# Moving the fifth expert block's second product ahead of a branch, and computing the third block in split precision

## Chip, cores and metric

One core of one Trainium2 chip runs the whole program. The metric is the device time of one execution in microseconds (us); lower is better. The kernel before takes 602.93 us in the median of three runs.

## What is computed

Attention over 4 batches and 8 heads feeds a first mixture of experts, and that feeds a second one. The change lies in the second one alone, whose 2304 tokens of 512 numbers are dealt to 8 experts of at most 288 tokens each:

```python
logits = x @ w_gate
for idx in np.argsort(-logits.flatten()):      # best (token, expert) pairs first
    tok, e = idx // E, idx % E
    if assigned[tok] < 0 and counts[e] < 288:
        assigned[tok] = e; counts[e] += 1
for e in range(8):
    h = np.maximum(x[assigned == e] @ w1[e], 0.0)
    out[assigned == e] = h @ w2[e]
```

## The kernel before

**Two strands.** After the first mixture (about 285 us into the span) two strands run interleaved until the end. The *search* settles the experts one after the other, in eight phases. A phase (`phase`) takes six steps to find the score at which an expert is full. Each step is a comparison `G` on VectorE (DVE), 18 small matmuls `pc` on TensorE (PE), a count `sat` and `an` on DVE, one small matmul `pa<-an` on PE and the next threshold `th` on DVE. A phase ends with the prefix count `pp` (PE) and `sc`, `sl`, `alive` (DVE). Then `ilist` makes the list of the expert's tokens (DVE `si`, `ol`, `OH`, `rh`, PE `pl`, DVE `li`, `ib`), and GpSimd (POOL) gathers those rows into `xg` (line 982). The last three experts first pass through `ahead` (DVE `mk`, `mksb`, PE `pk`), which sorts out tokens that need no computing, and through a small count `pz`, from which DVE works out a flag `zi`.

**Blocks.** The other strand computes the experts in the order in which the search settles them, block 0 to block 7. `first(m)` is x·w1 with ReLU: 8 groups (f) of 4 products of 128x128 by 128x288. `second(m)` is h·w2: 4 groups (d) of 8 such products. Blocks below `LATE` (0, 1 and 2) run in plain fp32. The trace has such a product as two MATMUL rows (`pa<-x,w1b`, `pa<-h,w2b`). From block `LATE` on, operands are split into a high and a low fp32r part (`xhs`/`xls`, `hhs`/`hls`, `w1hs`/`w1ls`, `w2hs`/`w2ls`), and a product is three fp32r matmuls. The split costs ScalarE (ACT) a copy and DVE a subtraction for each part: `sp1(m,k)` four times for w1, during `second(m-1)`; `sp2(m,k)` four times for w2, during `first(m)`; `xls` four times in `X(m,d)`, which brings the gathered rows of the next block into place by transposes `pt` during `second(m-1)`; `hls` eight times. Transposes `pt` and those of the outputs, `py`, share a pool of two PSUM buffers, and `pt` is free again when `xhs` and `xls` have read it.

**What sets the order.** All engines run their instructions in program order. A planner (`Search.tick`, `step`, `after`) sets that order when the program is built: it keeps a reckoned time of PE (`Q.pe`) and of DVE (`Q.dv`), and puts the next piece of the search in between block products when PE's reckoned time has come up to it. So PE's row of instructions says how many block products stand between two steps of the search.

**The branch.** `Q.until` finishes the search, `z=nc.values_load(K.zi...)` (line 1179) loads the flag on every engine, and `tc.If(z>1)` chooses `short()` when the last expert computes nothing and two others hold at most 160 tokens. These inputs take `short()`: it writes zero rows by five scatters from POOL, runs `second(4)` with `X`-like transposes `xin(5,d)` in between (lines 1119 to 1124), then blocks 5 and 6 in plain fp32 with 160 columns (lines 1132 and 1144), and ends. Loads of w1 and w2 for block 5 are issued by SyncE (SP) once the expert's number is out (`eb`); those for block 6 follow.

Of the kernel before, what the change touches and what calls it, by code (L numbers as in the profile page):

```python
# [7 lines left out]
F32 = mybir.dt.float32  # L8
# [11 lines left out]
E = 8  # L20
# [978 lines left out]

BUB=5  # L1000
FEW=160
LATE=3


def moe2(nc,tc,t,K,W,Q,yd,w1,w2,out):
    V=Q.V; G=nc.gpsimd; T=Q.T
    with ExitStack() as ctx:
        c=ctx.enter_context(tc.tile_pool(name="m2c",bufs=1))
        b2=ctx.enter_context(tc.tile_pool(name="m2b",bufs=2))
        acc=ctx.enter_context(tc.tile_pool(name="m2a",bufs=4,space=PSUM))  # L1010
        pst=ctx.enter_context(tc.tile_pool(name="m2p",bufs=2,space=PSUM))
        psr=ctx.enter_context(tc.tile_pool(name="m2r",bufs=2,space=PSUM))
        R=Q.B; tick=Q.tick; K.zi=None
# [3 lines left out]
        sw=[c.tile(x,F32R,name=f"{n}s") for n,x in (("w1h",[128,4,1024]),("w1l",[128,4,1024]),("w2h",[128,8,512]),("w2l",[128,8,512]))]  # L1017
# [5 lines left out]
        def sp1(m,k):  # L1023
            sp(0,Q.w1b[m%2],slice(k,k+1),k)
            if k==3: R[m].f1=True; Q.loads()
# [3 lines left out]
        def X(m,d):  # L1029
            r=R[m]  # L1030
            if d==0 and m<LATE: r.x=b2.tile([128,4,CAP],F32,name="x2",bufs=1)
            pt=pst.tile([128,288],F32,name="pt2",tag="t")
            for u in range(3): T.transpose(pt[:,96*u:96*u+96],r.xg[:,u,128*d:128*d+128],K.ident[:96,:96])
            if m<LATE: nc.scalar.copy(r.x[:,d],pt)
            else: nc.scalar.copy(xs[0][:,d],pt); Q.after(0.6); V.tensor_tensor(xs[1][:,d],pt,xs[0][:,d].bitcast(F32),op=ALU.subtract)
            tick()
# [14 lines left out]
        def mul(m,pa,z,k,sl,first,last):  # L1051

            if m<LATE:
                T.matmul(pa,(Q.w1b,Q.w2b)[z][m%2][:,k,sl],(R[m].x,hT)[z][:,k],start=first,stop=last); tick()
# [3 lines left out]
        def first(m):  # L1058
            r=R[m]; Q.blk=m
            for f in range(8):  # L1060

                if m==LATE and f>3: sp2(m,f-4)
                elif m>LATE and f%2==0: sp2(m,f//2)
                if m>0 and f in (1,2,3): O(m-1,f-1)
# [9 lines left out]
        def second(m):  # L1074
            r=R[m]

            nx=R[m+1] if m+1<E else None
            at=0; ws=0 if m+1>=LATE and nx is not None else 4
            for d in range(4):
                pa=acc.tile([128,288],F32,name="pa",tag="acc")  # L1080
                for k in range(8):
                    if nx is not None and at<4 and nx.xg is not None and nx.tx<=Q.pe and k%2: X(m+1,at); at+=1
                    if ws<4 and nx.l1 and k%4==0: sp1(m+1,ws); ws+=1
                    mul(m,pa,1,k,slice(128*d,128*d+128),k==0,k==7)
                nc.scalar.copy(yT[:,d],pa)
            r.f2=True; Q.loads()
            if nx is not None:
                Q.until(lambda: nx.xg is not None and nx.l1)
                while ws<4: sp1(m+1,ws); ws+=1
                Q.until(lambda: nx.l2)  # L1090
                if at<4 and nx.tx>Q.pe: Q.idle(nx.tx-Q.pe)
                while at<4: X(m+1,at); at+=1
        def short():


            T=nc.tensor
            CH=((0,96),(96,FEW-96))
            wv=[None,None]
            wv[0]=(Q.w1b[BUB%2],Q.w2b[0]); wv[1]=(Q.w1b[(BUB+1)%2],Q.w1b[BUB%2].rearrange("p k f -> p (k f)").rearrange("p (k f) -> p k f",k=8))
            ys=[]  # L1100
            def row(m,h,n,dd=range(4),pt=None):

                if pt is None: pt=pst.tile([96,512],F32,name="py2",tag="t")
                for d in dd: T.transpose(pt[0:n,128*d:128*d+128],yT[:,d,96*h:96*h+n],K.ident)
                return pt
            def to(m,h,n,pt):
                yn=b2.tile([96,512],F32,name="yn2",bufs=3)
                if n<96: G.memset(yn[n:96],0.0)
                nc.scalar.copy(yn[0:n],pt[0:n]); put(m,h,yn)
            xs_={}  # L1110
            def xin(m,d):
                if d==0: xs_[m]=b2.tile([128,4,CAP],F32,name="x2",bufs=1)
                pt=pst.tile([128,288],F32,name="pt2",tag="t")
                for u,(a,n) in enumerate(CH): T.transpose(pt[:,a:a+n],R[m].xg[0:n,u,128*d:128*d+128],K.ident[:n,:n])
                V_.tensor_copy(xs_[m][:,d,0:FEW],pt[:,0:FEW])
            V_=nc.vector
            for h in range(3): put(E-1,h,zr)
            for m in (BUB,BUB+1): put(m,2,zr)
            for d in range(4):
                pa=acc.tile([128,288],F32,name="pa",tag="acc")  # L1120
                for k in range(8):
                    if k==4: xin(BUB,d)
                    for y,(w,h_) in enumerate(((0,0),(0,1),(1,0))): T.matmul(pa,sw[2+w][:,k,128*d:128*d+128],hs[h_][:,k],start=k==0 and y==0,stop=k==7 and y==2)  # L1123
                nc.scalar.copy(yT[:,d],pa)
            for m in (BUB,BUB+1):
                w1_,w2_=wv[m-BUB]; x=xs_[m]
                for f in range(8):
                    if m==BUB:
                        if f in (1,2,3): to(m-1,f-1,96,row(m-1,f-1,96))
                    elif f in (1,2): to(m-1,f-1,CH[f-1][1],row(m-1,f-1,CH[f-1][1]))  # L1130
                    pa=acc.tile([128,288],F32,name="pa",tag="acc")[:,0:FEW]
                    for k in range(4): T.matmul(pa,w1_[:,k,128*f:128*f+128],x[:,k,0:FEW],start=k==0,stop=k==3)  # L1132
                    nc.scalar.activation(hT[:,f,0:FEW],pa,AF.Relu)
                if m==BUB:
                    e=R[m+1].e
                    for k in range(2): nc.sync.dma_start(wv[1][1][:,4*k:4*k+4],w2[bass.ds(e,1),512*k:512*k+512].rearrange("a (k p) f -> p (a k) f",p=128))
                pts=[]
                for d in range(4):
                    pa=acc.tile([128,288],F32,name="pa",tag="acc")[:,0:FEW]
                    for k in range(8):  # L1140
                        if m==BUB and k==4: xin(BUB+1,d)
                        if m>BUB and d==3 and k==2:
                            for u,(a,n) in enumerate(CH): pts.append(row(m,u,n,range(3)))
                        T.matmul(pa,w2_[:,k,128*d:128*d+128],hT[:,k,0:FEW],start=k==0,stop=k==7)  # L1144
                    nc.scalar.copy(yT[:,d,0:FEW],pa)
            yn=[b2.tile([96,512],F32,name="yn2",bufs=3) for _ in CH]
            G.memset(yn[1][CH[1][1]:96],0.0)
            for u,(a,n) in enumerate(CH):
                (nc.scalar.copy if u==0 else V_.tensor_copy)(yn[u][0:n,0:384],pts[u][0:n,0:384])
            for u,(a,n) in enumerate(CH):  # L1150
                row(BUB+1,u,n,(3,),pts[u])
                (nc.scalar.copy if u==0 else V_.tensor_copy)(yn[u][0:n,384:512],pts[u][0:n,384:512])
                put(BUB+1,u,yn[u])
        with tc.manual_schedule():
            Q.psum=lambda shape,name: psr.tile(shape,F32,name=name,tag="rc")
            Q.xgp=b2
            pw=[]
            def keep(n):

                if not pw: pw.append(acc.tile([128,128],F32,name="pw",tag="acc"))  # L1160
                for _ in range(n): nc.tensor.matmul(pw[0],K.ones,K.ones,start=True,stop=True)
            Q.keep=keep
            Q.until(lambda: R[0].xg is not None)
            Q.idle(IDLE)
            x0=[pool.tile([128,288],F32,name="pt2",tag=tag) for pool,tag in ((pst,"t"),(pst,"t"),(acc,"acc"),(acc,"acc"))]
            r=R[0]
            r.x=b2.tile([128,4,CAP],F32,name="x2",bufs=1)
            for u in range(3):
                for d in range(4): T.transpose(x0[d][:,96*u:96*u+96],r.xg[:,u,128*d:128*d+128],K.ident[:96,:96])
            for d in range(4): nc.scalar.copy(r.x[:,d],x0[d])  # L1170

            nc.scalar.copy(Q.w2b[0][0:1,0,0:1],r.x[0:1,3,0:1]); Q.x0=True; Q.loads()
            G.memset(zr,0.0)
            Q.keep=None
            for m in range(BUB-1): first(m); second(m)
            first(BUB-1)

            Q.until(lambda: K.zi is not None and R[BUB].l2 and R[BUB+1].l1)
        z=nc.values_load(K.zi[0:1,0:1],min_val=0,max_val=2)
# [1 line left out]
            with tc.manual_schedule(): short()  # L1181
        with few.Else():
            with tc.manual_schedule():
                second(BUB-1)
                for m in range(BUB,E-1): first(m); second(m)
            with tc.If(z>0) as cmp:
                with tc.manual_schedule():
                    for h in range(3): O(E-2,h)
            with cmp.Else():
                with tc.manual_schedule():  # L1190
                    first(E-1); second(E-1)
                    for h in range(3): O(E-1,h)
# [62 lines left out]
```

## Time and profile before

| | us |
|---|---|
| runs of the kernel before | 602.37, 602.93, 603.78; median 602.93 |
| the profiled execution | 605.14 |
| its span in the trace | 603.4, so 1.74 lie outside |
| `second(4)` and `xin(5)` after the branch | 535.62 to 552.35 of the span |
| blocks 5 and 6 and the end | 552.35 to 603.4 |

PE is busy for 541.6 us of the span, DVE for 350.0, ACT for 170.3, POOL for 111.6. The profile is read here as a time line: which instruction stands when on PE and DVE, and what the one waits for on the other. Times are us from the start of the span. A matmul row's length includes its way through the array; two matmuls in a row start closer together than they are long, so rates are taken from starts.

### The profile page before, as it was taken

What the parts mean: (1) busy time and instruction counts of PE and PEld (TensorE: products, weight loads), DVE (VectorE), ACT (ScalarE), POOL (GpSimd) and SP (SyncE); (2) the same over time, 40 slices, a digit from 0 to 9 for tenths busy, and PEclk for the clock granted to TensorE, in tenths of its full rate; (3) what the DMA queues carried; (4) which work ended last, traced back from release to release, by engine and by line L of the source; (5) the groups of instructions that cost most, each with busy time, mean ns of one, the idle gap of its engine ahead of it and who ended that gap; (6) DMA issues with size and microseconds to landing.
All of it is one profiled execution on the core that took longest, in us unless ns stands there. A gap on an engine that the chain in (4) does not pass through costs nothing.

```text
span 603.4 us, 10702 instructions
## 1 busy us (share of the span) xinstructions
PE 541.6 (90%) x4160; PEld 458.9 (76%) x4160; DVE 350.0 (58%) x1107; ACT 170.3 (28%) x310; POOL 111.6 (18%) x122
## 2 busy tenths in 40 slices
PE   0689996899999999899997999999999999859992
PEld 0579895898879987798775676767777899759992
DVE  8799879584328341484656365657567786830000
ACT  2244532252424342453000111211223262402120
POOL 4061701303110311000113020302120200262011
PEclk9998999899999999999997699999999899969997
DMA  9992733795403440000014440814432440197401
GB/s 267 307 263 60 255 140 112 231 331 192 172 36 87 141 176 35 15 1 1 33 56 171 144 167 14 323 42 175 160 111 89 165 154 2 39 311 270 162 28 30
DMA packets 54006, 82.46 MB, mean 137 GB/s; under 512 B 11904, under 2 KB 33408, under 8 KB 53936
## 3 DMA queue, kind: packets, MB, share of 16 engines
q1 hardware_dynamic: 38416, 58.82, 29.5%
q0 software_dynamic: 5088, 15.93, 8.4%
q10 hardware_dynamic: 10432, 6.82, 3.8%
q8 instruction: 39, 0.64, 0.4%
q14 instruction: 31, 0.25, 0.1%
HBM read 63.86 MB, written 17.70 MB: 135 GB/s over the span
## 4 chain that ended last, share of the span: by engine, by line
PE 67%; DVE 6%; ACT 2%; issue 2%; POOLq 0%; POOL 0%; ACTq 0%; DVEq 0%
PE pa L781 28%; PE pc L781 4%; PE pa L463 3%; PE pa L465 3%; PE pa L464 3%; PE pa L1144 3%; PE pa L383 3%; PE pa L1132 3%; PE pa L384 3%; PE pa L385 3%; PE pa L1123 3%; PE pt L781 1%; PE pg L431 1%; PE py L781 1%; PE pt L379 1%
## 5 line engine op out<-in xcount | busy, mean ns | idle before, releaser
L383 PE MATMUL pa<-xh,w1h 128*128 128x256 f32 (+1 forms) x192 | 58.7, 306 | 1.0 <-issue 0.6
L384 PE MATMUL pa<-xl,w1h 128*128 128x256 f32 (+1 forms) x192 | 57.6, 300 | 0.3 <-DVE xl L381 0.3
L385 PE MATMUL pa<-xh,w1l 128*128 128x256 f32 (+1 forms) x192 | 57.5, 299 | 0.0
L781 PE MATMUL pa<-h,w2b 128*128 128x288 f32 x192 | 55.5, 421 | 0.0
L1039 POOL DMA_INDIRECT out_dram<-yn,ib x19 | 19.5, 1027 | 146.6 <-ACT yn L1047 102.0
L781 PEld LDWEIGHTS pa<-h,w2b 128*128 128x128 f32 x192 | 33.5, 189 | 7.4 <-issue 0.7
L391 DVE SCALAR_TENSOR_TENSOR hl<-pa,hh 128x256 fp32r<-128x256 f32 (+1 forms) x48 | 21.6, 453 | 30.2 <-ACT hh L390 25.7
L781 PE MATMUL pa<-x,stage 128*128 128x288 f32 x128 | 39.0, 446 | 0.1
L383 PEld LDWEIGHTS pa<-xh,w1h 128*128 128x128 f32 x192 | 37.0, 193 | 2.4 <-issue 1.3
L384 PEld LDWEIGHTS pa<-xl,w1h 128*128 128x128 f32 x192 | 37.0, 193 | 0.6 <-DVE xl L381 0.5
L385 PEld LDWEIGHTS pa<-xh,w1l 128*128 128x128 f32 x192 | 37.1, 193 | 0.0
L982 POOL DMA_INDIRECT xg<-yd,ib x21 | 21.6, 1028 | 77.1 <-issue 47.8
L402 POOL DMA_INDIRECT yd<-y,idx x15 | 15.1, 1004 | 110.9 <-ACT y L398 93.0
L781 PEld LDWEIGHTS <-G 128*31 128x31 bf16 (+2 forms) x756 | 24.0, 102 | 14.8 <-DVE pre L781 6.4
L781 DVE TENSOR_TENSOR G<-b,th 128x372 bf16<-128x372 f32 (+2 forms) x70 | 33.1, 508 | 1.2
L390 ACT ACTIVATE hh<-pa 128x256 fp32r<-128x256 f32 (+1 forms) x48 | 19.7, 410 | 48.0 <-PE pa L385 47.2
L463 PE MATMUL pa<-w2h,hh 128*128 128x512 f32 (+1 forms) x80 | 33.0, 412 | 0.0
L465 PE MATMUL pa<-w2h,hl 128*128 128x512 f32 (+1 forms) x80 | 31.5, 393 | 0.0
L464 PE MATMUL pa<-w2l,hh 128*128 128x512 f32 (+1 forms) x80 | 31.3, 391 | 0.0
L781 PEld LDWEIGHTS pa<-x,stage 128*128 128x128 f32 x128 | 24.1, 202 | 5.6 <-ACT x L1170 0.3
L781 PE MATMUL pc<-g,G 128*31 128x8 bf16 (+2 forms) x756 | 27.8, 170 | 0.0
L781 DVE TENSOR_SCALAR_CACHE_REDUCE sat<-pc 31x8 f32<-31x8 f32 (+1 forms) x35 | 5.4, 155 | 36.6 <-PE pc L781 27.9
(385 smaller groups left out, 1286.6 us busy)
## 6 DMA issues: line engine op xcount, KB each, us to landing
stage<-in_moe_w_dram SPq DMA_DIRECT2D x18, 1024.0 KB, 6.3
w2b<-in_moe_w_dram SPq DMA_DIRECT2D x12, 1024.0 KB, 5.5
w1b<-in_moe_w_dram SPq DMA_DIRECT2D x8, 1024.0 KB, 5.2
yd<-z ACTq DMA_DIRECT2D x1, 4608.0 KB, 25.6
km<-in_k_dram SPq DMA_DIRECT2D x4, 1024.0 KB, 10.2
vm<-in_v_dram SPq DMA_DIRECT2D x4, 1024.0 KB, 10.8
xd<-xs SPq DMA_DIRECT2D x8, 512.0 KB, 2.6
qm<-in_q_dram SPq DMA_DIRECT2D x3, 1024.0 KB, 9.5
```

The source lines that it names most:

```text
L383: T.matmul(ps,wh,xh_,start=first,stop=False)
L384: T.matmul(ps,wh,xl_,start=False,stop=False)
L385: T.matmul(ps,wl,xh_,start=False,stop=last)
L390: A.activation(hh[:,f,s],pa,AF.Relu)
L391: V.scalar_tensor_tensor(hl[:,f,s],pa,0.0,hh[:,f,s].bitcast(F32),op0=ALU.max,op1=ALU.subtract)
L463: T.matmul(pa,hh[:,k,ts],W.w2h[:,k],start=(k==0),stop=False)
L464: T.matmul(pa,hh[:,k,ts],W.w2l[:,k],start=False,stop=False)
L465: T.matmul(pa,hl[:,k,ts],W.w2h[:,k],start=False,stop=(k==7))
L781: return f(*a,**k)
L982: nc.gpsimd.indirect_dma_start(out=B.xg[:,h],out_offset=None,in_=self.yd,in_offset=bass.IndirectOffsetOnAxis(ap=B.idx[:,h:h+1],axis=0),bou ...
L1039: s_=G.indirect_dma_start(out=out,out_offset=bass.IndirectOffsetOnAxis(ap=R[m].idx[:,h:h+1],axis=0),in_=src,in_offset=None,bounds_check=N- ...
L1123: for y,(w,h_) in enumerate(((0,0),(0,1),(1,0))): T.matmul(pa,sw[2+w][:,k,128*d:128*d+128],hs[h_][:,k],start=k==0 and y==0,stop=k==7 and y==2)
```

## The change

`LATE` goes from 3 to 2: block 2 is computed in split precision as well, so two blocks stay in plain fp32. And `second(4)` moves from behind the branch to ahead of it: it now goes through the planner, right after `first(4)` and ahead of `Q.until`, without transposes or splits for a next block. In `short()` only the four `xin(5,d)` are left of that loop; in the other arm a new helper `ready` does what `second(4)` did there for block 5.

```diff
-LATE=3
+LATE=2
...
         def second(m):
-            nx=R[m+1] if m+1<E else None
+            nx=R[m+1] if m+1<E and m!=BUB-1 else None
...
+            if nx is not None: ready(m+1,at,ws)
+        def ready(m,at,ws):
+            nx=R[m]
+            Q.until(lambda: nx.xg is not None and nx.l1)
+            while ws<4: sp1(m,ws); ws+=1
...
-            for d in range(4):
-                pa=acc.tile([128,288],F32,name="pa",tag="acc")
-                for k in range(8):
-                    if k==4: xin(BUB,d)
-                    for y,(w,h_) in enumerate(((0,0),(0,1),(1,0))): T.matmul(pa,sw[2+w][:,k,128*d:128*d+128],hs[h_][:,k],start=k==0 and y==0,stop=k==7 and y==2)
-                nc.scalar.copy(yT[:,d],pa)
+            for d in range(4): xin(BUB,d)
...
-            first(BUB-1)
+            first(BUB-1); second(BUB-1)
...
-                second(BUB-1)
+                ready(BUB,0,0)
```

The planner sets a new order from `second(1)` on. Three places show it.

PE in `second(1)`, where block 2's rows are transposed (`pt`) and the search's phase 4 takes its first step (`pc`). Before:

```order
L781 MATMUL pa<-h_12404,w2b 128x288 x2
L781 MATMUL pt_13377<-ident,xg_13095 128x96 x3
L781 MATMUL pa<-h_12404,w2b 128x288 x5
L781 LDWEIGHTS G
L781 MATMUL pc<-g,G 63x8
```

After:

```order
L781 MATMUL pa<-h_12404,w2b 128x288 x2
L781 MATMUL pt_13369<-ident,xg_13095 128x96 x3
L781 MATMUL pa<-h_12404,w2b 128x288 x16
L781 LDWEIGHTS G
L781 MATMUL pc<-g,G 63x8
```

Eleven plain products more stand ahead of that step; 23 of the stage's 32 are then done, before it was 12.

DVE behind the end of phase 4, from the phase's last update (`closed`) to the next phase's `eq`. Before:

```order
L781 TENSOR_TENSOR closed<-closed,eo 128x8
L781 SCALAR_TENSOR_TENSOR sc<-sb,pp_13669,w__947 128x18 x2
L781 TENSOR_TENSOR sl_967<-sc 128x18
L781 SCALAR_TENSOR_TENSOR sl_967<-sl_967 128x18
L781 SCALAR_TENSOR_TENSOR alive<-sl_967,alive 128x18
L781 TENSOR_REDUCE b<-LG_151 128x18
L781 TENSOR_TENSOR eq<-LG_151,b 128x144
```

After, from the same `b` on (ahead of `sc` stand two pairs of `hls` and `w2ls` more):

```order
L781 TENSOR_REDUCE b<-LG_151 128x18
L781 SCALAR_TENSOR_TENSOR hls<-pa,hhs 128x288
L781 TENSOR_TENSOR w2ls<-w2b,w2hs 128x1024
L781 SCALAR_TENSOR_TENSOR hls<-pa,hhs 128x288
L781 TENSOR_TENSOR w2ls<-w2b,w2hs 128x1024
L781 TENSOR_TENSOR eq<-LG_151,b 128x144
L781 SCALAR_TENSOR_TENSOR hls<-pa,hhs 128x288
L781 TENSOR_TENSOR w1ls<-w1b,w1hs 128x1024
L781 TENSOR_TENSOR xls<-pt_13827,xhs 128x288
L781 TENSOR_TENSOR xls<-pt_13839,xhs 128x288
```

The splits of block 2's second operand, of its hidden rows and of block 3's first operand now stand between the search's instructions, where nothing of that kind stood. On PE, 27 matmuls of `first(2)`, all 96 of `second(2)` with four `pt` after the 3rd, 9th, 15th and 21st, and 11 of `first(3)` now stand between this `pp` and the `pl` of the list that follows.

PE around the branch. Before (the search's last rows, the load of the flag, and the first products behind it; ahead of them stand all of `first(4)` and the end of phases 6 and 7):

```order
L781 MATMUL pz_14900<-kept,onesb 96x2
L1179 TENSOR_LOAD zi
L1180 COMPARE_AND_BRANCH
L1123 MATMUL pa<-hhs,w2hs 128x288
```

After (the last products of `second(4)`, the search's `pk`, then, with 18 `pl`, `pp`, `pz`, `pk` and 18 `pl` in between, the same end; behind the branch the transposes):

```order
L781 MATMUL pa<-hls,w2hs 128x288
L781 MATMUL pa<-hhs,w2ls 128x288
L781 LDWEIGHTS Ls
L781 MATMUL pk_15011<-mksb,Ls 128x1
```

```order
L781 MATMUL pz_15159<-kept,onesb 96x2
L1176 TENSOR_LOAD zi
L1177 COMPARE_AND_BRANCH
L1116 MATMUL pt_15246<-ident,xg_15092 128x96
L1116 MATMUL pt_15246<-ident,xg_15092 128x64
```

Before, phase 6's `pp` stood behind the first 12 of `first(4)`'s 96 matmuls. Now it stands behind 78 of `second(4)`'s 96, and behind the last 18 only rows of the search are left ahead of the branch.

## Rows read from the trace of the kernel before

**Rows 1.** The page's chain that ended last: shares of the span by engine.

```profile
PE 67%; DVE 6%; ACT 2%; issue 2%; POOLq 0%; POOL 0%; ACTq 0%; DVEq 0%
```

**Rows 2.** Time line of PE: start, length, line, operation, tiles, count; idle before.

```profile
413.18 0.74 PE L781 MATMUL pc<-g,G 128*63 128x8 bf16 x18
...
472.60 0.60 PE L781 MATMUL py<-ident,yT 128*96 128x128 f32 x4
...
511.11 0.19 PE L781 MATMUL pp<-sb,Ls 128*128 128x1 bf16 x2
...
540.12 0.30 PE L1123 MATMUL pa<-hhs,w2hs 128*128 128x288 f32 x1
...
541.71 0.29 PE L1123 MATMUL pa<-hhs,w2hs 128*128 128x288 f32 x1
```

**Rows 3.** The chain in order of time: start, length, engine, plain products' rows in `first(2)`.

```profile
437.22 3.88 PE pa L781 x16
```

**Rows 4.** Windows of block 3: bounds, length, busy time by engine, PEclk, DMA, GB/s.

```profile
477.60:478.60 1.00, 0.17 (x3) 0.03 (x1) 0.87 (x8) 0.00 (x0) 0.00 (x0) 1.00 0.71 213
478.60:482.00 3.40, 3.40 (x15) 3.33 (x16) 2.73 (x10) 0.99 (x2) 0.00 (x0) 0.51 0.01 2
```

**Rows 5.** Time line of DVE: the search's instructions, and those of a split.

```profile
407.01 0.39 DVE L781 SCALAR_TENSOR_TENSOR sc<-sb,pp,w__947 128x18 f32<-128x18 bf16 x2 [0.70 <-PE pp L781]
...
408.29 0.31 DVE L781 TENSOR_TENSOR eq<-LG,b 128x144 f32<-128x144 f32 x1
...
412.60 0.30 DVE L781 TENSOR_TENSOR ge<-g,r 128x144 f32<-128x144 bf16 x1
...
431.77 0.17 DVE L781 TENSOR_REDUCE cm<-pa 128x1 f32<-128x8 f32 x1 [0.64 <-PE pa L781]
...
433.84 0.16 DVE L781 TENSOR_TENSOR closed<-closed,eo 128x8 f32<-128x8 f32 x1
...
510.71 1.23 DVE L781 TENSOR_TENSOR w2ls<-w2b,w2hs 128x1024 fp32r<-128x1024 f32 x1 [0.46 <-ACT w2hs L1021]
511.85 0.45 DVE L781 SCALAR_TENSOR_TENSOR hls<-pa,hhs 128x288 fp32r<-128x288 f32 x1
512.22 0.39 DVE L781 SCALAR_TENSOR_TENSOR sc<-sb,pp,w__947 128x18 f32<-128x18 bf16 x2
```

**Rows 6.** Time line of DVE: the search's last instructions, ahead of the branch.

```profile
514.38 0.23 DVE L781 TENSOR_TENSOR_SCAN mksb<-rst,mk 128x36 bf16<-128x36 f32 x1
...
525.91 0.14 DVE L781 TENSOR_SCALAR z<-pz 96x1 f32<-96x1 f32 x1
...
526.60 0.17 DVE L781 CAST ib<-cdx 96x3 int32<-96x3 f32 x1
...
527.48 0.23 DVE L781 TENSOR_TENSOR_SCAN mksb<-rst,mk 128x36 bf16<-128x36 f32 x1
...
533.09 0.15 DVE L781 TENSOR_SCALAR z<-pz 96x1 f32<-96x1 f32 x1 [0.26 <-PE pz L781]
...
534.62 0.14 DVE L781 CAST zi<-few 1x1 int32<-1x1 f32 x1
```

**Rows 7.** Time line of PE behind the branch.

```profile
535.62 0.60 PE L1123 MATMUL pa<-hhs,w2hs 128*128 128x288 f32 x1 [2.57 <-DVE eb L781]
...
538.66 0.66 PE L1114 MATMUL pt<-ident,xg 96*128 96x96 f32 x2
...
552.35 1.25 PE L1132 MATMUL pa<-x,w1b 128*128 128x160 f32 x8
```

**Rows 8.** Window behind the branch, columns as in rows 4.

```profile
535.60:540.00 4.40, 4.38 (x17) 3.97 (x18) 0.32 (x1) 0.00 (x0) 2.97 (x4) 0.50 1.03 339
```

**Rows 9.** Time line of POOL: first gather of block 4, and of block 5.

```profile
444.17 1.00 POOL L982 DMA_INDIRECT xg<-yd,ib  x1 [4.77 <-issue]
...
527.55 0.99 POOL L982 DMA_INDIRECT xg<-yd,ib  x1 [9.39 <-issue]
```

**Rows 10.** DMA from 445.8 to 449.7: POOL's queue: packets, MB, share of 16 engines.

```profile
q0 software_dynamic: 192, 0.59, 50.9%
```

**Rows 11.** DMA from 532.3 to 538.2: SP's queue and POOL's.

```profile
q1 hardware_dynamic: 419, 1.28, 68.8%
q0 software_dynamic: 192, 0.59, 33.4%
```

More of the change, by code (lines that the diff above doesn't have):

```diff
@@ L1086, in second @@
             r.f2=True; Q.loads()
[L1087 to L1092, printed above, removed]
+            if nx is not None: ready(m+1,at,ws)
[3 more added lines that the diff above has]
+            while ws<4: sp1(m,ws); ws+=1
+            Q.until(lambda: nx.l2)
+            if at<4 and nx.tx>Q.pe: Q.idle(nx.tx-Q.pe)
+            while at<4: X(m,at); at+=1
         def short():
```

## Prediction

> **What bounds the kernel now.** The chain that ended last is read first: two thirds of it are PE [rows 1]. So far a shorter block would pay. But the time line of PE ahead of the branch shows another bound at that one place: PE comes out of the search's last rows idle, its first product behind the branch at 535.62 waiting for DVE [rows 7]. There the last wait to end is the search's: phase 6's prefix count at 511.11 [rows 2], the flag `zi` at 534.62, ending 534.76 [rows 6], and PE 0.86 later [rows 7]. Behind the branch PE runs 16.73 us of `second(4)` and transposes until block 5 starts at 552.35 [rows 7]. So the question is not what `second(4)` costs but when the search ends, and what PE can do until then and after. I work from one point that both orders share, the first step of phase 4 at 413.18 [rows 2], to phase 6's `pp`, from there to the flag, and from there to block 5's first product. All that follows that product stays as it is: 603.4 - 552.35 = 51.05.
>
> **Unit prices.** A plain product is two rows: 16 rows in 3.88 us [rows 3], so 0.485 a product. Twelve split matmuls lie between 540.12 and 541.71 [rows 2], 0.1325 each, three of them 0.40. Block 2 has 64 products, so PE saves 64 x 0.0875 = 5.6. A `w2ls` or `w1ls` holds DVE 1.14 (510.71 to 511.85), an `hls` 0.37 (511.85 to 512.22) [rows 5]; I take 0.4 for an `xls`, which is as large. Block 2's split puts 8 x 1.14 + 8 x 0.37 + 4 x 0.4 = 13.7 us on DVE, in the middle of the search.
>
> **Part 1: to phase 6's `pp`.** Before, 413.18 to 511.11 is 97.9 [rows 2]. In that stretch stood 20 plain products left of `second(1)` and 64 of block 2, and 192 + 12 split matmuls: 84 and 204. After, phase 4's first step stands 11 plain products later: 413.18 + 11 x 0.485 = 418.5. From there 9 plain products are left, and 192 (block 2) + 192 (block 3) + 96 + 78 (block 4) = 558 split ones. The 18 search steps, the three lists and the eight groups of `pt` are as many as before; two groups of output transposes come in, at 0.4 (between 0.35 and the 0.60 of the row [rows 2]). So 97.9 - 75 x 0.485 + 354 x 0.1325 + 0.8 = 109.2, and `pp` stands at 527.7. The added matmuls are on the path, since PE's order is fixed.
>
> That sum carries over the stalls of before. The one that is plain in the windows goes: at 477.6 PE was idle for 0.83 of a microsecond's window waiting for the search's list, and from 478.6 to 482.0 its granted clock was 0.51, the lower level [rows 4]: 0.8 + 1.7 = 2.5 off, 525.2. These come in:
> - In `second(1)`: four `w1ls` and four `xls` now stand ahead of or inside the stretch from `sc` (407.01) to the end of `ge` (412.90) [rows 5], 6.2 us. `ge` ends at 419.1, and `pc` starts 0.3 behind it [rows 2, 5], at 419.4, where PE would be at 418.5: 0.9. The first `w1ls` can also be late by ACT's copy, or fill the 0.70 in which DVE idled [rows 5]: 0 to 1.6, I take **1.1**. Queued behind that `pc` are all of PE's products.
> - In `second(2)`: from `cm` to the end of `closed` DVE takes 2.2 [rows 5], which puts the end of phase 4's `closed` some 0.7 ahead of `pp`. From there DVE's row has five `hls`, five split subtractions, `sc` to `b` with the `eq` (1.3 + 0.3 [rows 5]) and the first `xls`: 1.85 + 5.7 + 1.6 + 0.4 = 9.6, so that `xls` ends 8.9 behind `pp`. PE's third `pt` stands behind 27 + 15 split matmuls and two `pt`, 42 x 0.1325 + 0.6 = 6.2 behind `pp`, and must wait for that `xls`, since the pool has two buffers: **2.7**. Below: 0, if DVE starts earlier than I put it; above: 3.5.
> - An idle of that size can bring the clock down as at 478.6: 0 to 1.7, I take **1.0**.
>
> The gain of block 2, 5.6, is in the sum, and is nearly all taken back by these stalls. `pp` comes out at 525.2 + 1.1 + 2.7 + 1.0 = **530.0**, 18.9 later than before.
>
> **Part 2: from `pp` to the flag.** Before this took 23.65, with `hls`, `w2ls` and `first(4)` in between. After, DVE and PE have nothing else left but 18 matmuls, 2.4 us, so each link takes what it took where it was undisturbed: `pp` to `sc` 0.3 (as `pz` to `z` [rows 6]); `sc` to the end of `mksb` 512.22 to 514.61, 2.4 [rows 5, 6]; end of `mksb` to `z`, 527.71 to 533.09, 5.4 [rows 6]; the added `sc` and `sl` of phase 7 0.6; `z` to the end of the second `mksb`, 525.91 to 527.71, 1.8; again 5.4; `z` to the end of `zi`, 533.09 to 534.76, 1.7 [rows 6]. Together 17.6: the flag at 547.6, PE ready at **548.5**. PE is idle for some 15 us of this: the moved stage is spent by then.
>
> **Part 3: from the flag to block 5.** The rows of block 5 now meet PE at once. `ib` is out 0.3 + 2.4 + 5.4 + 0.6 + 0.9 = 9.6 behind `pp`, at 539.6. Before, `ib` started at 526.60 [rows 6], the first gather was issued at 527.55 [rows 9], and its queue moved all of block 5's 0.59 MB between 532.3 and 538.2 [rows 11], while SP's queue moved the weights. That is 11.5 behind `ib`, and the transposes at 538.66 [rows 7] came just in time, behind 12 matmuls. A gather with the queues quiet moved the same 0.59 MB by 449.7, 5.5 behind its first issue at 444.17 [rows 9, 10], against 10.6. After, weights and gather are issued by the same `eb` and `ib`, so they collide as before: 539.6 + 11.5 = **551.1**, 2.6 behind PE. Price between 0 and 2.6; I take the upper end, as it is the nearer row.
>
> The Trainium skill, page "DMA: Bandwidth & Descriptors", section "Anatomy of one DMA — SWDGE (gpsimd) path", gives a fixed cost of about 2.0 us and 436 GB/s for a single DMA; by it (an estimate) a gather of 0.2 MB lands 2.5 us behind its issue, and PE would not wait. The contended row speaks against that here, the quiet one for it. The rival below with the quiet gather is this rule.
>
> Then `xin(5)`: four pairs of transposes through two buffers at the lower clock (0.66 a pair [rows 7], a copy of some 0.3 and its handing over between the first and third, and the second and fourth) take 2.4 before block 5's first product, at 553.5. Before, the clock stayed at 0.50 for 4.4 us behind the branch [rows 8]; after, 2.0 of these fall on block 5's products and cost 1.0 (between 0 and 2.2). Effectively 554.5 against 552.35: **+2.2**. Weights for its second stage, put off with the rest, are needed some 10 us later and have that room.
>
> Span 605.6, execution 607.3 against the profiled 605.14. That execution lies 2.2 above the median of the runs; on the median, 602.93 + 2.2 = **605.1**.
>
> **Rivals.**
> 1. *No stall in `second(2)`.* DVE works ahead where I let it start late; the 2.7 and the 1.0 of clock go: 601.4. For: DVE idles 0.6 to 0.8 ahead of `cm` and `sc` in these steps [rows 5]. Against: its row holds 9.6 us of work where PE has 6.2. It decides from the point at which `xls` ends less than 6.2 behind `pp`. This is the side of faster.
> 2. *The gather is not slowed.* PE is then the last to come, at 548.5 instead of 551.1: 602.5. For: quiet row [rows 10]; against: [rows 11].
> 3. *More stalls.* Split blocks fill 100 us of the stretch instead of 40, DVE is the tighter engine in them, and each idle of PE may cost the clock again, 1.7 a time: two more, 608.3.
> 4. *The move does all that it can.* The search ends as it did and 16.7 us vanish behind it. Then block 5 waits only for the gather at 538.2: 540.6 and 1.0 of clock, 592. Against: the bare sum of PE's row, with no stall at all, has `pp` at 525.2, 14 later than before, so below 597 nothing is left.
>
> **How the numbers follow.** Forecast 0.50 (603.7 to 607), rival 1 0.19, rival 2 0.13, rival 3 0.15, rival 4 0.03. Some 0.2% (1.2 us) is what a measurement of this kernel can tell from no change: 601.7 to 604.1 is the same. Faster: rivals 4 and most of 1, a little of 2 and of the forecast, 0.24. Same: the rest of 1 and 2 and the forecast's lower end, 0.26. Slower 0.50. The range leaves out rival 4, the lower end of 1 and half of 3: 600.8 to 608.3; the forecast's own is 603.7 to 607.
>
> **What would show it.** Phase 6's `pp` at 528 to 532; a third `pt` in `second(2)` that waits 2 us or more for `xls`; PE idle for over 12 us ahead of the branch; the flag 17 to 18.5 behind `pp`; the first transposes behind the branch released by the gather, not by the flag; block 5's first products at the lower clock. If `pp` stands ahead of 527.8, the kernel is faster and part 1 is wrong; if the transposes start 0.9 behind the flag, part 3 is.

## The result, and the profile after

| | us | ratio to before | 95% interval |
|---|---|---|---|
| before | 602.93 | | |
| changed kernel (median of five runs, 608.56 to 614.94) | 609.51 | 1.0143 | 1.0107 to 1.0179 |
| predicted | 605.1 (600.8 to 608.3) | | |

The changed kernel is slower. The sign is the forecast one; the size is not: +6.6 where +2.2 was predicted, outside the range. (The recorded ratio is not the quotient of the two medians, which is 1.0109.) The first profiled execution of the changed kernel happened to be its longest, 614.94. The rows below are therefore from a second trace of the same kernel (label `again`, execution 610.82, span 609.0). The traces differ already ahead of anything that the change touches: phase 3's prefix count stands between 403.63 and 408.28 in them. So places are compared by their distance within a trace. The page of the first one has, as the chain's shares (of before: [rows 1]):

```profile
PE 65%; DVE 8%; issue 2%; ACT 2%; POOLq 0%; POOL 0%; ACTq 0%; DVEq 0%
```

DVE has a larger share of the chain than before (8% for 6%), which fits the bare tail of the search shown below. Time line of PE in the second trace (answering [rows 2]): phase 4's first step, three of PE's waits, phase 6's prefix count.

```profile
418.23 0.74 PE L781 MATMUL pc<-g,G 128*63 128x8 bf16 x18
...
449.76 0.47 PE L781 MATMUL pt<-ident,xg 96*128 96x96 f32 x3 [2.26 <-DVE xls L781]
...
467.33 0.16 PE L781 MATMUL pa<-an,onesb 63*128 63x1 bf16 x1 [0.55 <-DVE sat L781]
...
510.21 0.16 PE L781 MATMUL pa<-an,onesb 63*128 63x1 bf16 x1 [0.35 <-DVE sat L781]
...
534.67 0.20 PE L781 MATMUL pp<-sb,Ls 128*128 128x1 bf16 x2
```

Windows of the same trace, columns as in [rows 4] (busy time of PE, PE's weight loads, DVE, ACT and POOL, then the granted clock): behind each of the three waits, and behind the branch (before: [rows 8]).

```profile
450.30:453.80 3.50, 3.50 (x18) 3.49 (x17) 1.95 (x4) 1.71 (x4) 0.00 (x0) 0.51 0.70 262
467.30:470.80 3.50, 3.47 (x16) 3.31 (x15) 1.93 (x7) 0.57 (x2) 2.69 (x3) 0.52 0.23 61
511.70:515.10 3.40, 3.40 (x17) 3.40 (x16) 3.20 (x14) 0.41 (x1) 0.00 (x0) 0.52 0.01 2
552.80:555.50 2.70, 2.64 (x9) 1.42 (x9) 0.97 (x3) 0.00 (x0) 1.93 (x2) 0.50 1.04 335
555.50:559.80 4.30, 4.30 (x19) 4.21 (x19) 0.33 (x1) 0.88 (x2) 2.95 (x4) 0.52 1.06 328
```

PE is busy throughout the first three, at the lower of the clock's two levels (1.2 of 2.4 GHz): about 1.7 us lost in each. In the half-microsecond windows from 418.2 to 537 the lost time adds up to 5.1, and it is 5.1 in the first trace too, at the same three places.

Time line of PE from the last list ahead of the branch to block 5 (answering [rows 7]):

```profile
544.75 0.19 PE L781 MATMUL pk<-mksb,Ls 128*128 128x1 bf16 x2 [2.37 <-DVE mksb L781]
...
547.78 0.66 PE L781 MATMUL pl<-rh,OH 128*32 128x27 bf16 x18 [2.81 <-DVE rh L781]
549.95 0.16 PE L781 MATMUL pz<-kept,onesb 96*96 96x2 bf16 x1 [1.51 <-DVE kept L781]
552.79 2.77 PE L1116 MATMUL pt<-ident,xg 96*128 96x96 f32 x8 [2.68 <-DVE eb L781]
555.49 1.97 PE L1129 MATMUL pa<-x,w1b 128*128 128x160 f32 x6
```

The transposes stand 18.12 behind the prefix count and wait for the flag alone: they start 1.11 behind the start of `zi` (551.68). The gather had come, but only just. POOL's queue between 545.0 and 551.9 in this trace:

```profile
q0 software_dynamic: 110, 0.39, 18.1%
```

That is nearly all of two of the gather's three transfers, and the transposes use only those two (160 rows of 288). The packets of 4 bytes that close the second one are recorded up to 552.66, 0.13 ahead of the first transpose.

### The profile page after: what moved, and what is told of

It is laid out like the page before. It is cut to its first block, busy times and chain, and to the rows that moved or that the text cites. A ratio compares the mean times of both kernels' runs of the same rounds, so it can differ in the third digit from the quotient of the medians.

```text
span 613.1 us, 10876 instructions
## 1 busy us (share of the span) xinstructions
PE 542.0 (88%) x4224; PEld 467.3 (76%) x4224; DVE 363.5 (59%) x1127; ACT 177.5 (29%) x318; POOL 110.7 (18%) x122
## 4 chain that ended last, share of the span: by engine, by line
PE 65%; DVE 8%; issue 2%; ACT 2%; POOLq 0%; POOL 0%; ACTq 0%; DVEq 0%
PE pa L781 29%; PE pc L781 4%; PE pa L1129 3%; PE pa L463 3%; PE pa L465 3%; PE pa L464 3%; PE pa L1141 3%; PE pa L383 3%; PE pa L385 3%; PE pa L384 3%; DVE w2ls L781 1%; PE pg L431 1%; PE py L781 1%; PE pt L781 1%; PE pl L781 1%
## 5 line engine op out<-in xcount | busy, mean ns | idle before, releaser
L781 PE MATMUL pa<-h,w2b 128*128 128x288 f32 x128 | 36.4, 419 | 0.0
L781 PE MATMUL pa<-xhs,w1hs 128*128 128x288 f32 x96 | 31.2, 325 | 0.0
L781 PE MATMUL pa<-xhs,w1ls 128*128 128x288 f32 x96 | 30.5, 317 | 0.0
L781 PE MATMUL pa<-xls,w1hs 128*128 128x288 f32 x96 | 30.2, 314 | 0.0
L781 PE MATMUL pa<-hhs,w2hs 128*128 128x288 f32 x96 | 30.1, 314 | 0.0
L781 PE MATMUL pa<-hhs,w2ls 128*128 128x288 f32 x96 | 29.5, 307 | 0.0
```

The source lines that it names most:

```text
L781: return f(*a,**k)
```

## The experiments

Ratios are to the kernel before, timed beside each variant on the same chip.

**A second trace.**

> The changed kernel once more, for a second trace of it: the first trace came from its longest execution, 614.94 us. Expected 608.5 to 610.5. If the three falls of the clock between phase 4 and phase 6 (3.5 us each at 0.50 in the first trace) belong to the kernel, at least two of them stand here too; if they are what made that execution long, there is one or none, and phase 6's prefix count stands near 531 instead of 538. The first hidden rows of block 5 on ScalarE, which came in fits there (561.35, 564.34, 569.34), follow PE within 1 us if that was an accident of the execution, and lag again if it belongs to the order behind the branch.

Measured 611.18 (two runs; 1.0151, 1.0096 to 1.0206), a little above what was expected. All three falls of the clock stand here again, and the prefix count is 116.4 behind phase 4's first step (117.4 in the first trace). So they are no accident of the first execution, though not every execution has all three (below). ACT lags here too: it takes up block 5's second hidden row at 561.92, for products that ended near 560.4, and idles 2.55 more ahead of its next copy.

**The two edits apart.**

```diff
-LATE=3
+LATE=2
```

> Block 2 split, second(4) left behind the branch. Theory 1: the 13.7 us that the split puts on DVE delay the search, while PE's work ahead of the branch shrinks by 5.6, so that PE has nothing left for phase 6's last five steps and for the tail of 17.6 us, and second(4)'s 16.7 us come on top: 609.5 + 16.7 less some 3 to 6 for steps that are closer together without products in between, 618 to 624. Theory 2 (the split is about even on the path, 5.6 saved against 4.6 to 6 of stalls and clock; it is the move that costs): 602 to 606.

Measured 618.24 (1.0256, 1.0209 to 1.0303): theory 1. Phase 6's last steps in its trace, time line of PE:

```profile
524.94 0.65 PE L781 MATMUL pc<-g,G 128*31 128x8 bf16 x18 [1.12 <-DVE G L781]
527.11 0.65 PE L781 MATMUL pc<-g,G 128*31 128x8 bf16 x18 [1.12 <-DVE G L781]
529.29 0.65 PE L781 MATMUL pc<-g,G 128*31 128x8 bf16 x18 [1.12 <-DVE G L781]
...
534.31 0.19 PE L781 MATMUL pp<-sb,Ls 128*128 128x1 bf16 x2 [1.78 <-DVE sb L781]
```

No block product stands between the steps any more. The split alone costs 15.7 us, and the move gives back 7 to 9 of these.

```diff
-LATE=2
+LATE=3
```

(against the changed kernel)

> second(4) ahead of the branch, block 2 in plain fp32 as before. Theory 1: the search runs as before (phase 6's prefix count at 511, the last pz near 533), the 96 matmuls of second(4) fill the waits of the tail (45 of them between pk, pl and pz, where PE idled 1.71, 2.81 and 1.43 before) and 51 stand behind the last pz, 6.8 us, so that the flag has long come: transposes near 540.5, block 5 near 542.5 at the full clock, 9 to 10 us earlier than before: 592 to 596. Theory 2 (the move costs, by a cold clock and by work behind the branch that loses its cover): 603 to 606.

Measured 601.06 (0.9985, 0.9948 to 1.0022): between both theories, so both missed something. Up to the transposes theory 1 holds: phase 6's prefix count is at 510.38, PE waits nowhere in the tail for more than 0.54, and the transposes stand at 539.37. Then a new wait opens. Time line of all engines:

```profile
538.26 0.96 POOL L1039 DMA_INDIRECT out_dram<-zr,ib  x1 [0.45 <-issue]
539.37 0.89 PE L1116 MATMUL pt<-ident,xg 96*128 96x96 f32 x4
...
543.42 0.92 POOL L1039 DMA_INDIRECT out_dram<-zr,ib  x1 [0.30 <-DMA xg<-yd,ib]
545.96 0.40 ACT L1085 COPY yT<-pa 128x288 f32<-128x288 f32 x1 [9.05 <-remote]
546.04 0.56 DVE L1117 COPY x<-pt 128x160 f32<-128x160 f32 x2 [11.48 <-remote]
546.42 1.36 PE L1116 MATMUL pt<-ident,xg 96*128 96x96 f32 x4 [6.16 <-DVE x L1117]
```

And a window behind that wait:

```profile
546.40:552.20 5.80, 5.78 (x22) 5.11 (x23) 0.84 (x3) 0.89 (x2) 0.24 (x1) 0.50 0.91 368
```

PE's first two pairs of transposes end at 540.26, and the last product of `second(4)` at 539.5. Yet ACT takes up that product at 545.96 and DVE the transposes at 546.04. "Remote" means that the view found no instruction ending where the signal came. The trace's semaphore records say why: PE's counter, on which both wait, takes no step between 536.42 and 545.88, and then four within 0.11 us. So it is the signals that are late, by some 6 us, not the two engines. They come through 1.5 us behind the end of POOL's eight indirect transfers (three gathers, five scatters of zero rows). The wait then costs the clock as well (0.50 for 5.8 us).

**PE kept busy in the tail.**

```diff
+            pw.clear(); Q.keep=keep
             Q.until(lambda: K.zi is not None and R[BUB].l2 and R[BUB+1].l1)
+            keep(24); Q.keep=None
```

> The changed kernel with matmuls of no use on PE wherever the plan sees it wait in the tail (19, 5, 26, 38 and 10 of 128x128 between pk, pl, pp and pz, 24 behind the last pz), the result not read. If the lower clock behind the branch costs what the first trace shows (eight transposes in 2.79 us, block 5's first 3.75 us at 0.50), it is 2.0 to 3.0 faster than the changed kernel: 606.5 to 607.5. If the wait for the flag behind them (1.7 to 2.7 us) brings the clock down all the same, no change: 609 to 610.

Measured 611.28 (1.0169, 1.0118 to 1.0219): nothing won. Time line of PE behind the branch, and two windows:

```profile
553.13 1.98 PE L1116 MATMUL pt<-ident,xg 96*128 96x96 f32 x8 [1.32 <-issue]
```

```profile
553.10:555.00 1.90, 1.81 (x8) 1.10 (x8) 0.94 (x3) 0.00 (x0) 1.32 (x2) 1.00 0.99 296
555.00:558.50 3.50, 3.49 (x14) 2.99 (x14) 0.36 (x2) 0.30 (x1) 2.52 (x3) 0.54 1.07 353
```

The transposes now run at the full clock, but the clock falls right behind them, and block 5's first products pay. From the transposes to the end it takes 56.2, as in `again`. The fall is put off, not avoided.

**The 2.26 us wait.**

```diff
-... and nx.tx<=Q.pe and k%2: X(m+1,at); at+=1
+... and nx.tx<=Q.pe and (k%2 if m!=2 else k==1): X(m+1,at); at+=1
```

> The changed kernel with the four pt of second(2) behind its 3rd, 27th, 51st and 75th matmul instead of the 3rd, 9th, 15th and 21st; nothing else in PE's row moves. The third pt, which waited 2.26 for xls, then stands 36 matmuls (4.8 us) later. Theory: that idle and the clock's fall behind it (1.7) are on the path, phase 6's prefix count comes 3 to 4 us earlier and the time is 606 to 608. Rival: DVE sets the search's pace there, the next step waits for DVE instead and nothing is won: 610 to 611.

Measured 605.79 (1.0032, 1.0006 to 1.0057): as the theory said, and in the search somewhat more. The first step is at 420.05; then, in the time line of PE, and in windows at the three places where the clock fell before:

```profile
465.45 0.16 PE L781 MATMUL pa<-an,onesb 63*128 63x1 bf16 x1 [0.56 <-DVE sat L781]
...
530.00 0.20 PE L781 MATMUL pp<-sb,Ls 128*128 128x1 bf16 x2
```

```profile
449.00:454.00 5.00, 4.94 (x37) 4.68 (x37) 5.00 (x9) 2.97 (x5) 0.00 (x0) 1.00 0.99 366
465.00:471.00 6.00, 5.55 (x54) 5.15 (x53) 4.88 (x15) 2.82 (x5) 4.47 (x4) 1.00 0.24 69
507.00:516.00 9.00, 8.98 (x91) 8.33 (x90) 7.66 (x26) 3.76 (x7) 0.00 (x0) 1.00 0.08 25
```

The stretch is 109.95 instead of 116.44: one wait of 2.26 and its fall (1.7) go, and the two later falls do not happen either, although the wait of 0.56 stands there as it did. Five traces have the order with that wait (both of the changed kernel, `split_only`, `warm` and `after_zeros_later`): the fall behind the 2.26 is in all of them, those behind 0.55 and 0.35 in the first three only. So of the 6.5 only some 4.0, the wait and its own fall, are shown to come from the moved `pt`. Nor is the length of a single wait what decides: in `again` PE waits 0.38 and 0.31 some 15 us earlier, and the clock stays up until 450; in the first trace it does so behind a wait of 0.61 at 477.85 (1.00 from 477 to 484). Time line of PE, and a window, in `again`:

```profile
431.05 0.16 PE L781 MATMUL pa<-an,onesb 31*128 31x1 bf16 x1 [0.38 <-DVE sat L781]
```

```profile
430.50:450.00 19.50, 16.37 (x150) 15.04 (x149) 15.30 (x50) 10.37 (x17) 1.85 (x2) 1.00 0.62 215
```

What decides stays open.

**Half of block 2's weight splits on POOL.**

```diff
-            (V if Q.gens or k%2 else G).tensor_tensor(lo,...)
+            (V if k%2 or Q.gens and m!=LATE else G).tensor_tensor(lo,...)
```

> The changed kernel with half of block 2's weight splits (w1ls and w2ls for even k, 4 of 8) on POOL instead of DVE. Theory 1: the load that the split puts on DVE (13.7 us, of it 4.6 taken away here) is what puts the search late; its plan and its run shift earlier by some 4 to 7, phase 6's prefix count stands near 529: 603 to 607. Rival: the load on DVE is not what counts, or POOL's own slower subtraction stands in its place (DVE and PE wait for w1ls and w2ls): 609 or more.

Measured 611.43 (1.0173, 1.0096 to 1.0251): nothing won, but it does not settle what it was made for. Time lines of POOL and DVE:

```profile
442.93 2.41 POOL L1022 TENSOR_TENSOR w2ls<-w2b,w2hs 128x1024 fp32r<-128x1024 f32 x1 [0.95 <-ACT w2hs L1021]
...
443.30 3.12 DVE L781 TENSOR_TENSOR w2ls<-w2b,w2hs 128x1024 fp32r<-128x1024 f32 x1
...
447.51 1.21 DVE L781 TENSOR_TENSOR w2ls<-w2b,w2hs 128x1024 fp32r<-128x1024 f32 x1
```

POOL needs 2.41 for what takes DVE 1.21, and DVE's own subtraction beside it took 3.12: it ends 1.1 after POOL's. DVE was not relieved, it was held. The Trainium skill, page "SBUF — State Buffer", section "Who interferes with whom", has this rule: a DVE instruction with two inputs in SBUF contends with a GpSimd one that reads SBUF, and whoever issues first holds the port for its whole instruction. The rows agree: POOL issued first, at 442.93 against 443.30.

**Late signals: where the zero rows stand.** The five scatters are put off to block 5's second stage, in three kernels:

```diff
-            for h in range(3): put(E-1,h,zr)
-            for m in (BUB,BUB+1): put(m,2,zr)
+            zp=[(E-1,0),(E-1,1),(E-1,2),(BUB,2),(BUB+1,2)]
...
                     for k in range(8):
+                        if m==BUB and k==0:
+                            for _ in range(1+d//3): put(*zp.pop(0),zr)
```

With the move alone:

> The kernel with the move alone, and the five scatters of zero rows, which POOL issued right behind the branch, put off to block 5's second stage (one ahead of each group of products, two ahead of the last). In the move alone ACT and DVE learn only at 545.9 of matmuls that PE ended at 539.5 to 540.3, and POOL's last scatter of the row ended at 544.3. Theory: signals between engines come late while POOL issues scattered transfers back to back. Then the wait of 6.16 goes, block 5 starts near 541.5 and at the full clock: 592 to 595. Rival: it is the weights' traffic (SP's queue moves block 6's w1 until 550) or code behind the branch that is late, and the wait stays: 600 to 602.

Measured **590.94** (0.979, 0.9739 to 0.9841), below the theory's range. Time line of all engines behind the branch, and at the scatters' new place:

```profile
538.12 1.88 PE L1116 MATMUL pt<-ident,xg 96*128 96x96 f32 x8
...
538.68 0.69 DVE L1117 COPY x<-pt 128x160 f32<-128x160 f32 x2 [5.37 <-DMA w2b<-in_moe_w_dram]
...
539.93 1.35 PE L1128 MATMUL pa<-x,w1b 128*128 128x160 f32 x8
...
550.89 0.91 POOL L1039 DMA_INDIRECT out_dram<-zr,ib  x1 [0.59 <-issue]
...
552.09 0.30 ACT L1129 ACTIVATE h<-pa 128x160 f32<-128x160 f32 x1 [2.63 <-PE pa L1142]
```

The wait is gone, and the clock stays at 1.00 until PE's work ends. SP's queue moved 2.28 MB of weights between 538 and 546, against 1.76 in the move alone, so it was not their traffic that held the signals. Code loading does not tell the two kernels apart either: one packet just behind the branch in each (at 538.3 here, at 539.5 there). Where the scatters stand now, ACT's last hidden row comes late (2.63), but there PE has products that need nobody.

With the changed kernel:

> The changed kernel with the same putting off of the five scatters. Block 5's first stage took 12.4 to 13.2 us in it, against 10.0 before; some 2.0 of this is the lower clock, the rest late signals to ACT. Theory: 0.5 to 1.5 us faster than the changed kernel, 608 to 610, and the first hidden rows on ACT follow PE within 0.5. Rival (traffic of the weights or code loading): no change, 609.5 to 611, ACT late as before.

Measured 609.02 (1.0122, 1.0064 to 1.0179). On ACT it is as expected (its third to seventh hidden row idle 0.46 to 0.78 us, which is PE's pace); in the time the difference is too small to tell. Block 5's first stage still takes 12.1 from 551.01, since the clock is low there.

With the kernel before:

> The kernel before with the five scatters of zero rows put off to block 5's second stage. In its trace the late signals of PE (up to 1.8 us, between 541 and 546) fall into second(4), whose groups of 24 matmuls run on with four PSUM buffers, and PE waits for nobody there. Theory: no change, 602 to 603.5. If late signals cost the kernel before as well, it is faster by 1 or more: 600 to 602.

Measured 603.02 (1.0013, 0.9982 to 1.0044): no change. Behind the branch `second(4)` had covered the late signals.

And the dose, in the move alone: two scatters left behind the branch, three put off.

```diff
+            for _ in range(2): put(*zp.pop(0),zr)
...
-                            for _ in range(1+d//3): put(*zp.pop(0),zr)
+                            for _ in range(d>0): put(*zp.pop(0),zr)
```

> The move alone, with two of the five scatters of zero rows left right behind the branch and three put off. With five, POOL's string of transfers ended at 544.3 and signals came through at 545.9; with none PE did not wait. Theory: signals come through some 1.5 us behind the last transfer of the string, here near 541 to 542.5, so that PE waits 1 to 3 us for the first x copies instead of 6.16: 593 to 598. Rival: what held the signals is not POOL's string but something that happens to end when it does; then it is either 591 or 601.

Measured 596.47 (0.9921, 0.9891 to 0.9952). Time line of all engines:

```profile
537.45 0.95 POOL L1039 DMA_INDIRECT out_dram<-zr,ib  x1 [0.51 <-issue]
...
539.38 0.56 DVE L1117 COPY x<-pt 128x160 f32<-128x160 f32 x2 [7.10 <-PE pt L1116]
...
539.75 1.36 PE L1116 MATMUL pt<-ident,xg 96*128 96x96 f32 x4 [1.77 <-DVE x L1117]
```

The string ends at 538.40, PE's counter steps at 539.22, 0.8 later, and PE's wait goes with the string's length: 6.16, 1.77, none for five, two and no scatters; 601.06, 596.47, 590.94.

A string does not hold every signal, though. In `again` the same eight transfers stand between 551.78 and 561.82, and PE's counter steps nine times in them, with 2.9 us as the longest gap; DVE's first copy of block 5's rows starts at 553.72, right behind its transposes. In the first trace the longest gap is 5.7 (560.74 to 566.46). Why the move alone has one of 9.5 is not shown.

**The split without its stalls.** Both mends in the changed kernel (`pt` spread, scatters put off):

> The changed kernel with both mends: the pt of second(2) spread, and the scatters put off. If the two losses found so far were all that the split of block 2 costs, it would stand with the move alone and late scatters, at 591 less up to 5.6. Theory: the split's load on DVE puts the search later against PE's work, so that the tail of 17.6 us stays bare behind phase 6's prefix count (near 529): 602 to 605.

Measured 606.09 (1.0049, 1.0017 to 1.0081): the theory, though 1.1 above its range. The prefix count stands at 530.07, no fall of the clock is left ahead of 534, and the tail is bare. It is 15.2 slower than the move with the same late scatters.

The same, with the planner not reckoning block 2's splits:

```diff
-            (V if Q.gens or k%2 else G).tensor_tensor(lo,...)
+            (nc.vector if m==LATE else V if Q.gens or k%2 else G).tensor_tensor(lo,...)
...
-            else: ...; Q.after(0.6); V.tensor_tensor(xs[1][:,d],...)
+                if m>LATE: Q.after(0.6)
+                (V if m>LATE else nc.vector).tensor_tensor(xs[1][:,d],...)
...
-                    Q.after(0.6); V.scalar_tensor_tensor(hs[1][:,f],...)
+                    if m>LATE: Q.after(0.6)
+                    (V if m>LATE else nc.vector).scalar_tensor_tensor(hs[1][:,f],...)
```

> As split_spread_zeros, but the planner does not reckon block 2's splits in DVE's time (they run on DVE all the same). PE's row then has the search's steps as early as in the kernel before, and 40 to 60 of second(4)'s matmuls behind phase 6's prefix count. If DVE itself is what makes the search late, PE now waits for it in block 2 and 3 (10 us or more in all, and the clock falls): 600 to 612. If only the plan was too careful, PE waits little and the saving of block 2 (5.6) shows: 585 to 592.

Measured 605.78 (1.0073, 1.0036 to 1.0111). Time line of PE, from phase 3's prefix count on:

```profile
403.63 0.19 PE L781 MATMUL pp<-sb,Ls 128*128 128x1 bf16 x2
...
415.77 0.64 PE L781 MATMUL pl<-rh,OH 128*32 128x18 bf16 x18 [2.77 <-DVE rh L781]
...
448.94 0.63 PE L781 MATMUL pl<-rh,OH 128*32 128x18 bf16 x18 [2.23 <-DVE rh L781]
...
494.12 0.47 PE L781 MATMUL pt<-ident,xg 96*128 96x96 f32 x3 [1.01 <-DVE xls L781]
...
524.17 0.20 PE L781 MATMUL pp<-sb,Ls 128*128 128x1 bf16 x2
```

The same two prefix counts in `split_spread_zeros`:

```profile
408.03 0.19 PE L781 MATMUL pp<-sb,Ls 128*128 128x1 bf16 x2
...
530.07 0.20 PE L781 MATMUL pp<-sb,Ls 128*128 128x1 bf16 x2
```

The tail is now full of products, but from phase 3's prefix count to phase 6's are 120.5 us, only 1.5 less than 122.0: between 412 and 545 PE waits 8.8 us for DVE and loses 5.6 to the clock. The price has only changed its place. In the move with the same late scatters the two counts are 102.8 apart (406.37 to 509.20). So under either plan the split sets the search back by 18 to 19 us, by the plan's order in one and by PE's waits for DVE in the other. That no order exists in which the split of block 2 pays is not shown.

## Why the prediction was wrong in size

From phase 4's first step to the end, the prediction had 605.6 - 419.6 = 186.0 (419.6 is its 418.5 and the 1.1 of stall). The second trace has 190.8. Up to that step it is 1.4 ahead of the forecast, 0.8 of it by its own earlier start (405.92 for 406.75 at phase 3's prefix count).

| stretch | predicted | measured | difference |
|---|---|---|---|
| first step of phase 4 to phase 6's `pp` | 110.4 | 116.4 | +6.0 |
| `pp` to the transposes behind the branch | 21.1 | 18.1 | -3.0 |
| transposes to block 5's first product | 2.4 | 2.7 | +0.3 |
| from there to the end | 52.1 | 53.5 | +1.4 |

Errors of either sign partly cancel here: with the tail as forecast, the total would have missed by 3.0 more.

- **Part 1, the stall ahead of phase 4's first step: not there.** 1.1 predicted; `pc` follows the products without idle. From phase 3's prefix count to it are 12.3 us, 6.4 before; of the 5.9 the eleven products are 5.3, and the four `pt`, which stand farther apart, are the rest.
- **Part 1, the bare sum: right.** 106.7 predicted; measured 116.4 less 4.4 of PE's waits and 5.1 of clock, 107.0. The eleven products and the search's place in them came as the order said.
- **Part 1, the third `pt`: right.** 2.7 predicted, 2.26 measured, released by `xls`; so rival 1 falls. `spread` shows the wait to be on the path.
- **Part 1, the clock: the step that failed.** The term was 1.0 for one idle; it measured 5.1: the fall behind that idle cost its full 1.7, and two more followed waits of 0.55 and 0.35 that the sum did not have. Not every execution pays all of it: `warm` and `after_zeros_later`, with the same order there, have the first fall alone, 1.7. I had taken a middle value where [rows 4] had the whole one. Rival 3 described just this, with the price right (its sum is 608.5, not 608.3), and was given 0.15. Seven small waits, 2.1 together and the two just named among them, were missed as well.
- **Part 2: right.** 18.5 predicted, 18.1 measured, and PE was idle for 13.2 of it.
- **Part 3, the gather: wrong.** The transposes need two of its three transfers, 0.39 MB. Nearly all of this was in 8.3 behind `ib` (543.59 to 551.9), before 8.4 (526.60 to 535.0), and its closing packets at 552.66. I had priced all three, at 11.5 (538.2 less 526.60 is 11.6). So the gather came no later than the flag: rival 2's outcome, but not for the reason it gave, since the queue was not quiet.
- **Part 3, the clock behind the branch: too small.** 1.0 predicted; the lower clock lasted 4.3 us of block 5's products, 2.2 lost, the upper end of what was allowed. `warm` shows that idling products in the tail do not help.
- **Not seen at all.** The lateness of PE's signals while POOL issues its string of transfers. It costs the changed kernel little: one wait of PE for ACT, 1.0, in the first trace, none in the second. It took from the move alone nearly all that it gained.

The prediction also treated the two edits as one. Apart, they differ: the split alone costs 15.7; the move alone makes no difference clear of its interval (-1.5), and 12.1 less once the scatters are out of its way. Its rival 4, "the move does all that it can", forecast 592; that is about what the move comes to without the split and with late scatters (590.94). The argument against it, "below 597 nothing is left", held for both edits together only.

## What to carry to other kernels

Price a faster stage on the engine that feeds the serial chain, not only on the one that it relieves: here an estimated 5.6 us saved on PE (by the prediction's prices) put 13.0 more on DVE (busy 363.0 in `again`, 350.0 before), and even without the two stalls that were mended phase 6's prefix count came 19.2 later behind phase 3's. When a stage moves out from behind a branch, ask what it covered there: not only its own time, but the clock's recovery and whatever makes handovers between engines late (here the string of scatters). And where edits come together, time each alone.

## What the hardware showed that was not expected

- In the move alone PE's signals to ACT and DVE came up to 6.3 us late while POOL issued indirect transfers back to back, and came through 0.8 to 1.5 us behind the last of them. The length of the lateness followed the number of transfers, and its place followed theirs. In the changed kernel a string of the same length let some signals through. By what path it holds them, the runs do not show.
- The granted clock fell to 0.50 for about 3.4 us behind a wait of PE of 2.26 us in all five traces that have it, and behind waits of 0.55 and 0.35 in three of them. Behind other waits of 0.31 to 0.69 in these traces it stayed at 1.00.
- A subtraction on POOL (2.41) beside one on DVE stretched DVE's from 1.21 to 3.12.
